# Three rotating PSUM tiles and eight score groups in an attention-plus-MLP kernel

## The chip, the core and the metric

The kernel runs on one core of a Trainium2 chip. The metric is device time in microseconds (us) of one execution. Five engines run their own instruction queues in order: TensorE (PE in the profile), VectorE (DVE), ScalarE (ACT), GpSimd (POOL) and SyncE (SP, which here only issues DMAs).

## The reference

Eight batches of 12 heads, 448 tokens, head size 64, go through an attention with normed q and k; its output, 3584 tokens of 768, goes through a two-layer MLP with a tanh GELU. Cut to what matters:

```python
def rmsnorm(x, g):
    return x / np.sqrt(np.mean(x * x, axis=-1, keepdims=True) + 1e-06) * g
scores = np.matmul(rmsnorm(q, g_q), rmsnorm(k, g_k).transpose(0, 1, 3, 2)) / np.sqrt(64)
attn = np.exp(scores - np.max(scores, axis=-1, keepdims=True))
attn = attn / (np.sum(attn, axis=-1, keepdims=True) + 1e-09)
x = np.matmul(attn, v).transpose(0, 2, 1, 3).reshape(8 * 448, 768)
h = x @ w_in                                    # 768 -> 2048
return gelu_tanh(h) @ w_out                     # 2048 -> 768
```

## The kernel before

The kernel walks over the batches. Everything is bf16 in the matmuls and float32 in PSUM. The instructions of each engine run in the order in which the Python code emits them (`manual_schedule`, L67); only waits between engines are added to it.

**Heads and units.** Twelve heads are three chunks `c` of four heads (`NCH = 3`). The 448 keys of a chunk are seven blocks `t` (`NT = 7`). A *unit* (L261) is one chunk and one block: four matmuls of 64x64 weights and 448 columns that run side by side in the four quarters of the array (a *set* below), which fill a PSUM tile `sc` of two banks, and one exponential on ACT (L274) that reads the tile and writes `ex[:, t]`. An attention has 21 units.

**Key sums.** The softmax sums go over keys. `key_sums` (L280) adds the `ex` blocks of a chunk on DVE: for the second block `es = ex0 + ex1` (L290), for the fourth and sixth `e2 = ex + ex` (L295) and `es += e2` (L296), for the seventh `es += ex` (L292). From batch 2 on all seven blocks are added so; for batch 1 chunks 0 and 2 add five, chunk 1 none. Then `products(b, c, 0)` (L298) multiplies what is left with ones on PE (one set where all was added), which gives the sums in a two-bank region `o`. `turned` (two transposes, L324) and `recips` (a reciprocal L330 and a transpose L331) turn them into `rb` on DVE.

**x.** `products(b, c, 1)` multiplies `v` with `ex` on PE (seven sets, also into `o`), and `quad_x` (L335) multiplies the result with `rb` on DVE into `xT`, one instruction per bank.

**The MLP.** `mm1` (L343) and `mm1_pair` (L404) make `h` from `xT` and `w_in` with 128x128 weights and 448 columns; ACT applies the GELU. `mm2` (L361) makes an output tile of 128 rows and 384 columns with 16 matmuls; the tile is then copied from PSUM by DVE (L391, `osb<-o`, called the *copy* below) and stored by SP.

**PSUM** has eight banks here: `ps_s` two tiles of two banks (`sc` and the pairs `hh` of the MLP, in turn), `ps_o` two banks (`o`, used by every sums and x product), `ps_m` two single banks (`mm`: `mm1`, `mm2`, transposes).

**The order in an attention** (L435) is written out: the 21 units go in 11 groups of two (the last has one), and a list `m2` of `mm2` matmuls of the batches before is dealt out between them: `first` 16 behind the first group, `last` 18 at the end, two beside each x product, the rest spread evenly, 112 in all (96 in the first such attention). After group 4 come the sums of chunk 0, after group 5 its x, after groups 8 and 9 those of chunk 1. Side work is hung to group numbers (`side`): sums of squares `total`, the gain of the keys `gain`, the inverse roots `rsqrt`, DMA issues. In each group the order of emission is: side work, units, the key sums of the previous group's second unit, a product, the `mm2` matmuls with their copies, and then the key sums of this group's first unit. At the end (L476 to L486) stand the last `mm2` matmuls, the sums of chunk 2, the first half of the MLP's first pair (`early`: inner chunks 0 to 3, which need the x of chunks 0 and 1), the x of chunk 2 and its multiplication, the second pair, and the `late` halves, which need the x of chunk 2. Then 72 `mm1` matmuls (L348) close the batch.

The very first attention (batch 0, `first_attention`, L488) has an order of its own. `attention` runs for batches 1 to 7.

Of the kernel before, what the change touches and what calls it, by code (L numbers as in the profile page):

```python
# [8 lines left out]
F32 = mybir.dt.float32  # L9
# [8 lines left out]
def kernel(  # L18
# [11 lines left out]
    nc = tc.nc  # L30
# [26 lines left out]
    xp = ctx.enter_context(tc.tile_pool(name="xp", bufs=2))  # L57
    gp = ctx.enter_context(tc.tile_pool(name="gp", bufs=1))
    op = ctx.enter_context(tc.tile_pool(name="op", bufs=3))
    ps_s = ctx.enter_context(tc.tile_pool(name="ps_s", bufs=2, space=bass.MemoryType.PSUM))  # L60
    ps_o = ctx.enter_context(tc.tile_pool(name="ps_o", bufs=1, space=bass.MemoryType.PSUM))
    ps_m = ctx.enter_context(tc.tile_pool(name="ps_m", bufs=2, space=bass.MemoryType.PSUM))

    ident = consts.tile([128, 128], BF16)
    make_identity(nc, ident)
# [190 lines left out]
    def gain(b, c):  # L256
        nc.vector.tensor_scalar(kT[:, c], kT[:, c], gcol[:, 0:1], None, op0=ALU.mult)
# [3 lines left out]
    def unit(b, c, t):  # L261

        if (b, c) not in exs:
            exs[b, c] = exq.tile([P, NT, 2, S], BF16, tag="ex", name="ex")
        ex = exs[b, c]
        sc = ps_s.tile([128, 2, 512], F32, tag="sc", name="sc")
        for a in range(2):
            rs = slice(a * D, (a + 1) * D)
            for r in range(2):
                nc.tensor.matmul(  # L270
                    sc[r * R:(r + 1) * R, a, :S], kT[rs, c, t, r], qT[b][rs, c, :, r],
                    start=True, stop=True,
                )
        nc.scalar.activation(ex[:, t], sc[:, :, :S], AF.Exp, scale=scale, bias=shift)  # L274
# [5 lines left out]
    def key_sums(b, c, t):  # L280

        n = added(b, c)
        if t > n or t == 0:
            return
        ex = exs[b, c]
        if t == 1:
            ess[b, c] = exq.tile([P, 2, S], BF16, tag="es", name="es")
        es = ess[b, c]
        if t == 1:
            nc.vector.tensor_add(es, ex[:, 0], ex[:, 1])  # L290
        elif t == n and n % 2 == 0:
            nc.vector.tensor_add(es, es, ex[:, t])  # L292
        elif t % 2:
            e2 = exq.tile([P, 2, S], BF16, tag="e2", name="e2")
            nc.vector.tensor_add(e2, ex[:, t - 1], ex[:, t])  # L295
            nc.vector.tensor_add(es, es, e2)  # L296

    def products(b, c, what, part=0, parts=1):  # L298

        if part == 0:  # L300
            oas[what] = [o[:, :S] for o in oall]
            if b == 0 and c + 1 == NCH and not what:
                oas[what] = [
                    ps_m.tile([128, 512], F32, tag="mm", name="os")[:, :S] for r in range(2)
                ]
        o = oas[what]
        es = [exs[b, c][:, t] for t in range(NT)]
        if not what and added(b, c):
            es[:added(b, c) + 1] = [ess[b, c]]
        n = len(es)  # L310
        for i in range(n * part // parts, n * (part + 1) // parts):
            for r in range(2):
                rs = slice(r * R, (r + 1) * R)
                for a in range(2):
                    nc.tensor.matmul(  # L315
                        o[r][a * D:(a + 1) * D],
                        vb[b % 2][rs, 2 * c + a, i] if what else ones[rs], es[i][rs, a],
                        start=(i == 0), stop=(i == n - 1),
                    )
# [15 lines left out]
    def quad_x(b, c):  # L335
        if c == 0:
            xT[b] = xp.tile([128, HP, S], BF16, tag="xT", name="xT")
        for r in range(2):
            nc.vector.tensor_mul(xT[b][:, 2 * c + r], oall[r][:, :S], oas["rb"][:, r])  # L339

# [63 lines left out]
    def mm1_pair(i, cs=range(HP), b=0, js=range(2)):  # L404

        if cs[0] == 0 and js[0] == 0:
            hs1[i] = ps_s.tile([128, 2, 512], F32, tag="sc", name="hh")
        h = hs1[i]
        for j in js:
            f = 2 * i + j  # L410
            for c in cs:
                nc.tensor.matmul(  # L412
                    h[:, j, :S], win[:, c, f * 128:(f + 1) * 128], xT[b][:, c],
                    start=(c == 0), stop=(c == HP - 1),
                )
        if cs[-1] == HP - 1 and js[-1] == 1:
            nc.scalar.activation(  # L417
                g[:, 2 * i:2 * i + 2, (b % 2) * S:(b % 2 + 1) * S], h[:, :, :S],
                AF.Gelu_apprx_tanh
            )  # L420
# [14 lines left out]
    def attention(b, m2, quota, side):  # L435

        units = [(c, t) for c in range(NCH) for t in range(NT)]
        groups = [units[i:i + 2] for i in range(0, len(units), 2)]
        first, last, beside = 16, 18, 2
        sums_at, x_at = {4: 0, 8: 1}, {5: 0, 9: 1}  # L440
        free = [i for i in range(1, len(groups) - 1) if i not in x_at]
        spread = quota - first - last - beside * len(x_at)
        given = 0

        def upto(k):
            nonlocal given
            while given < k:
                m2.pop(0)()
                given += 1

        before = []
        for i, group in enumerate(groups):
            for fn in side.get(i, ()):
                fn()
            for c, t in group:
                unit(b, c, t)
            for c, t in before:
                key_sums(b, c, t)
            if i in x_at:
                products(b, x_at[i], 1)  # L460
                quad_x(b, x_at[i])
                upto(given + beside)
            elif i in sums_at:
                products(b, sums_at[i], 0)
                turned()
            if i == 0:
                upto(first)
            elif i in free:
                n = spread * (free.index(i) + 1) // len(free) - spread * free.index(i) // len(free)
                upto(given + n // 2)  # L470
                if i in sums_at:
                    recips()
                upto(given + n - n // 2)
            key_sums(b, *group[0])
            before = group[1:]
        nc.scalar.preload_act_table_set(GELU_SET)  # L476
        upto(quota)

        c = NCH - 1
        products(b, c, 0)  # L480
        turned()
        mm1_pair(0, early, b)
        products(b, c, 1)
        recips()
        quad_x(b, c)
        mm1_pair(1, early, b)  # L486

# [166 lines left out]
    for b in range(B):  # L654
        m1, side = [], []
        if b == 0:

            m1 = [(0, lambda: total(1, 1, "q"),
                   lambda: total(1, 1, "k"), lambda: total(1, 2, "q"), lambda: total(1, 2, "k"),
                   lambda: rsqrt_newton(1), lambda: normed_both(1, 1, nc.gpsimd)),  # L660
                  (3, lambda: loads(2, 0)),
                  (4, lambda: transposed(1, 1), lambda: normed_both(1, 0, nc.vector),
                   lambda: normed_both(1, 2, nc.vector), lambda: loads(2, 1)),
                  (5, lambda: loads(2, 2),
                   lambda: square(2, 0, "q", nc.gpsimd),
                   lambda: square(2, 0, "k", nc.gpsimd)),
                  (5, lambda: trans(1, 0)),
                  (7, lambda: trans(1, 2))]
            side += [(0, lambda: total(2, 0, "q"), lambda: total(2, 0, "k")),
                     (2, lambda: gain(1, 1))]  # L670

            for c, slots in ((1, (5, 6)), (2, (7, 8))):
                for n, slot in zip("qk", slots):
                    side += [(2 * c - 1, lambda c=c, n=n: square(2, c, n, nc.gpsimd)),
                             (slot, lambda c=c, n=n: total(2, c, n))]
        elif b + 1 < B:

            m1.append((0, lambda: gpsimd_waits(ess[b, NCH - 1][:1, 0, :1])))
            for c in range(NCH):
                m1 += [(0, lambda c=c: normed_both(b + 1, c, nc.gpsimd)),  # L680
                       (4 * c + 4, lambda c=c: transposed(b + 1, c))]
            m1 += [(9, lambda: gain(b + 1, 0)), (14, lambda: gain(b + 1, 1))]
            side.append((3, lambda: gain(b + 1, 2)))
        if 0 < b and b + 2 < B:
            m1 += [(4, lambda: loads(b + 2, 1)), (8, lambda: loads(b + 2, 2))]
            for c, at in ((0, 4), (1, 9)):
# [22 lines left out]
            break  # L709
        nc.scalar.preload_act_table_set(EXP_SET)  # L710
        if b + 2 < B:
            side += [(10, lambda: rsqrt(b + 2)),
                     (0 if b else 2, lambda: load_v(b + 2, 0, HP))]
            if b + 3 < B:
                side.append((1, lambda: loads(b + 3, 0)))
        attention(b + 1, m2, 96 if b == 0 else 112, plan(*side))


# [28 lines left out]
```

## Time and profile before

| what | value |
|---|---|
| median of three runs | 425.52 us (425.33 to 425.61) |
| the profiled execution, its own time | 423.37 us |
| its span in the profile | 421.6 us |
| PE busy | 405.7 us, 96% of the span |
| ACT busy | 274.9 us, 65% |
| DVE busy | 259.8 us, 62% |
| POOL busy | 124.3 us, 29% |
| exponentials (L274) | 168, mean 1004 ns |
| copies of output tiles (L391) | 51, mean 550 ns |
| key-sum additions (L290, L292, L295, L296) | 116, 608 to 625 ns each |
| batch 2: its first units to those of batch 3 | 105.98 to 154.37 us |

The profile shows one execution. In its timeline view a line gives the start, the time, the engine, the line of the kernel, output and inputs, and how many instructions were merged; brackets give the idle time before it and what ended that. Matmuls overlap in the array, so the time from the start of one to the start of the next is what counts, not the time of one. The batches 2 to 7 repeat with a period of 48.39 us; batch 2 stands for them below.

### The profile page before, as it was taken

How to read it: one execution, taken by the hardware profiler on the slowest of the kernel's cores; microseconds unless marked ns; L12 is line 12 of the kernel's file. 1: busy time of each engine (PE TensorE's matmuls, PEld its weight loads, DVE VectorE, ACT ScalarE, POOL GpSimd, SP SyncE). 2: the span in 40 equal slices, each digit the busy share in tenths (PEclk: the TensorE clock that was granted, in tenths of full speed). 3: DMA queues.
4: the chain of work that ended last, by engine and by line, in shares of the span. 5: the costliest groups of instructions: out<-in, count | busy, mean ns of one | idle time of the engine just before them, and what ended most of it. 6: DMA issues, size and time to landing. Idle time of an engine off the chain costs nothing.

```text
span 421.6 us, 8029 instructions
## 1 busy us (share of the span) xinstructions
PE 405.7 (96%) x3321; PEld 205.7 (49%) x3321; DVE 259.8 (62%) x430; ACT 274.9 (65%) x364; POOL 124.3 (29%) x98
## 2 busy tenths in 40 slices
PE   5879999999999999999999999999999999999995
PEld 2336554545444544455444554445445454445563
DVE  4887947945689357973689455992589504891010
ACT  5885468838876587838877478747878348754300
POOL 5793515292202640063301840054400900000000
PEclk9998999999999999999999999999999999999999
DMA  7999999589521946249511958239411621130033
GB/s 261 208 256 243 218 192 280 96 205 264 78 62 41 241 79 181 76 104 294 98 39 39 215 129 191 64 83 268 64 46 39 125 45 38 39 75 3 0 75 76
DMA packets 65316, 54.06 MB, mean 128 GB/s; under 512 B 37376, under 2 KB 60288, under 8 KB 65280
## 3 DMA queue, kind: packets, MB, share of 16 engines
q1 hardware_dynamic: 52992, 41.66, 38.0%
q0 software_dynamic: 12128, 11.80, 17.7%
q8 instruction: 26, 0.43, 0.4%
q10 hardware_dynamic: 160, 0.10, 0.1%
q14 instruction: 10, 0.08, 0.1%
HBM read 45.61 MB, written 11.01 MB: 134 GB/s over the span
## 4 chain that ended last, share of the span: by engine, by line
PE 86%; ACT 9%; DVE 2%; POOL 2%; issue 1%; DMA 1%; DVEq 0%; ACTq 0%; POOLq 0%
PE o L368 32%; PE h L348 23%; PE hh L412 12%; PE o L315 9%; PE sc L270 8%; ACT ex L274 5%; ACT L710 2%; DVE ss L139 1%; POOL sq L134 1%; PE tp L228 1%; ACT g L354 1%; DMA rawq<-in_q_dram 1%; POOL win L544 1%; PE os L315 0%; DVE nrmk L210 0%
## 5 line engine op out<-in xcount | busy, mean ns | idle before, releaser
L274 ACT ACTIVATE ex<-sc,shift 128x896 bf16<-128x896 f32 x168 | 159.2, 1004 | 33.3 <-PE sc L270 31.9
L368 PE MATMUL o<-wout,g 128*128 128x384 bf16 x896 | 159.3, 327 | 0.0
L368 PEld LDWEIGHTS <-g 128*128 128x128 bf16 x896 | 81.3, 98 | 71.3 <-issue 23.3
L348 PE MATMUL h<-xT,win 128*128 128x448 bf16 x504 | 96.5, 352 | 0.0
L139 DVE TENSOR_REDUCE ss<-sq 128x14 f32<-128x896 f32 (+1 forms) x43 | 44.4, 1039 | 55.6 <-ACT sq L132 51.6
L348 PEld LDWEIGHTS <-win 128*128 128x128 bf16 x504 | 49.3, 98 | 46.0
L354 ACT ACTIVATE g<-h 128x448 bf16<-128x448 f32 x84 | 45.6, 543 | 28.2 <-PE h L348 23.1
L391 DVE COPY osb<-o 128x384 f32<-128x384 f32 x51 | 28.0, 550 | 58.3 <-PE o L368 58.0
L270 PE MATMUL sc<-qT,kT 64*64 64x448 bf16 x672 | 53.7, 366 | 4.7 <-ACT ex L274 3.5
L417 ACT ACTIVATE g<-hh 128x896 bf16<-128x896 f32 x22 | 19.3, 915 | 57.1 <-PE hh L412 57.1
L412 PE MATMUL hh<-xT,win 128*128 128x448 bf16 x264 | 52.9, 353 | 0.3 <-ACT g L417 0.3
L557 POOL COPY mark<-es 1x1 bf16<-1x1 bf16 x6 | 1.1, 177 | 139.7 <-DVE es L292 139.7
L210 POOL TENSOR_TENSOR nrmq<-rawq,rinv 128x896 bf16<-128x896 f32 x21 | 35.5, 1689 | 17.8 <-DVE o L195 11.9
L315 PE MATMUL o<-ex,vb 64*64 64x448 bf16 x672 | 38.1, 357 | 1.4 <-DVE st L324 1.4
L412 PEld LDWEIGHTS <-win 128*128 128x128 bf16 x264 | 24.6, 98 | 26.1 <-issue 5.0
L270 PEld LDWEIGHTS <-kT 64*64 64x64 bf16 x672 | 17.5, 104 | 37.1 <-issue 33.8
L210 POOL TENSOR_TENSOR nrmk<-rawk,rinv 128x896 bf16<-128x896 f32 x19 | 31.9, 1679 | 0.0
L324 DVE STREAM_TRANSPOSE st<-o 128x448 f32<-128x448 f32 x46 | 27.0, 625 | 6.8 <-PE o L315 6.7
L339 DVE TENSOR_TENSOR xT<-o,rb 128x448 bf16<-128x448 f32 x48 | 27.6, 618 | 4.7 <-PE o L315 4.2
L134 POOL TENSOR_TENSOR sq<-rawq 128x896 f32<-128x896 f32 x9 | 15.6, 1733 | 50.5 <-DVE ss L139 37.8
L315 PEld LDWEIGHTS <-vb 64*64 64x64 bf16 x672 | 20.4, 108 | 15.1 <-issue 4.6
L295 DVE TENSOR_TENSOR e<-ex 128x896 bf16<-128x896 bf16 x38 | 23.2, 611 | 7.0 <-ACT ex L274 7.0
(77 smaller groups left out, 266.0 us busy)
## 6 DMA issues: line engine op xcount, KB each, us to landing
out_dram<-osb SPq DMA_DIRECT2D x54, 192.0 KB, 2.7
rawq<-in_q_dram SPq DMA_DIRECT2D x23, 448.0 KB, 4.4
rawk<-in_k_dram SPq DMA_DIRECT2D x23, 448.0 KB, 4.9
vb<-in_v_dram POOLq DMA_DIRECT2D x8, 672.0 KB, 6.7
win<-in_moe_w_in_dram POOLq DMA_DIRECT2D x8, 384.0 KB, 13.7
wout<-in_moe_w_out_dram POOLq DMA_DIRECT2D x2, 1536.0 KB, 29.4
rawq<-in_q_dram SPq DMA_DIRECT2D x2, 224.0 KB, 2.6
rawk<-in_k_dram SPq DMA_DIRECT2D x2, 224.0 KB, 4.2
```

What stands on the lines that cost most here:

```text
L139: nc.vector.reduce_sum(sss[b][:, c, "qk".index(n), hs], sqs[n, b, c][:, hs], axis=AX.X)
L210: eng.tensor_mul(nrms[n, b, c][:, ts].rearrange("p t a d -> p a t d"), raws[n, b, c][:, :, ts], root[:, :, ts].to_broadcast([P, 2, m, D]),)
L270: nc.tensor.matmul(sc[r * R:(r + 1) * R, a, :S], kT[rs, c, t, r], qT[b][rs, c, :, r], start=True, stop=True,)
L274: nc.scalar.activation(ex[:, t], sc[:, :, :S], AF.Exp, scale=scale, bias=shift)
L315: nc.tensor.matmul(o[r][a * D:(a + 1) * D], vb[b % 2][rs, 2 * c + a, i] if what else ones[rs], es[i][rs, a], start=(i == 0), stop=(i == n ...
L324: nc.vector.transpose(st[:, r].rearrange("p a b -> p (a b)"), oas[0][r])
L339: nc.vector.tensor_mul(xT[b][:, 2 * c + r], oall[r][:, :S], oas["rb"][:, r])
L348: nc.tensor.matmul(h[:, :S], win[:, c, f * 128:(f + 1) * 128], xT[b][:, c], start=(c == 0), stop=(c == HP - 1),)
L354: nc.scalar.activation(g[:, f, (b % 2) * S:(b % 2 + 1) * S], h[:, :S], AF.Gelu_apprx_tanh)
L368: nc.tensor.matmul(o[:, :HD], g[:, f, i * 128:(i + 1) * 128], wout[:, f, half * HD:(half + 1) * HD], start=(f == 0), stop=(f == nf - 1),)
L391: nc.vector.tensor_copy(part, o[:, :HD])
L412: nc.tensor.matmul(h[:, j, :S], win[:, c, f * 128:(f + 1) * 128], xT[b][:, c], start=(c == 0), stop=(c == HP - 1),)
```

## The change

The PSUM pools `ps_s` and `ps_o` live until the first call of `attention` and are then closed; in their place come three tiles of two banks that go round in one fixed turn (`rounds`). Whoever asks for a two-bank tile (`pair`) gets the one whose last use lies furthest back: a unit's scores, a chunk's sums, a chunk's x, and the MLP pairs. `quad_x` then is one instruction over both banks.

The 21 units go in eight groups of 3, 3, 3, 2, 2, 3, 2 and 3. The sums of chunk 0 come after group 3, its x after group 4, the sums of chunk 1 after group 6. The x of chunk 1 moves to the end: there the sums of chunk 2, the x of chunk 1 and the x of chunk 2 follow one another on PE, and the first pair's early half comes behind them. 22 `mm2` matmuls stand behind the first group and 18 at the end; the rest is dealt evenly to the six groups between (12 each, 9 or 10 in the first such attention). At the end of a group the key sums of all its units but the last are emitted (in the last group those of the last unit too, ahead of the last 18 `mm2`). For chunk 2 the fifth, sixth and seventh blocks are added one by one. The group numbers of the side work are adapted: `gain(b + 1, 2)` from 3 to 2, `rsqrt` from 10 to 7, and in the first such attention `gain(1, 1)` from 2 to 1, the squares of batch 2 from 1 and 3 to 1 and 2, their totals from 5 to 8 to 4 to 6, and the load of `v` from 2 to 1.

```diff
-    ps_s = ctx.enter_context(tc.tile_pool(name="ps_s", bufs=2, space=bass.MemoryType.PSUM))
-    ps_o = ctx.enter_context(tc.tile_pool(name="ps_o", bufs=1, space=bass.MemoryType.PSUM))
     ps_m = ctx.enter_context(tc.tile_pool(name="ps_m", bufs=2, space=bass.MemoryType.PSUM))
+    start = ctx.enter_context(ExitStack())
+    ps_s = start.enter_context(tc.tile_pool(name="ps_s", bufs=2, space=bass.MemoryType.PSUM))
+    ps_o = start.enter_context(tc.tile_pool(name="ps_o", bufs=1, space=bass.MemoryType.PSUM))
+    rounds = []
+
+    def pair(name):
+        if not rounds:
+            return ps_s.tile([128, 2, 512], F32, tag="sc", name=name)
+        rounds.append(rounds.pop(0))
+        return rounds[-1]
...
-        sc = ps_s.tile([128, 2, 512], F32, tag="sc", name="sc")
+        sc = pair("sc")
...
-        elif t == n and n % 2 == 0:
+        elif t == n and n % 2 == 0 or c + 1 == NCH and t > 3:
             nc.vector.tensor_add(es, es, ex[:, t])
...
-        if part == 0:
+        if part == 0 and rounds:
+            o = oas["o", what] = pair("o")
+            oas[what] = [o[:, r, :S] for r in range(2)]
+        elif part == 0:
             oas[what] = [o[:, :S] for o in oall]
...
+        if rounds:
+            nc.vector.tensor_mul(
+                xT[b][:, 2 * c:2 * c + 2], oas["o", 1][:, :, :S], oas["rb"]
+            )
+            return
         for r in range(2):
             nc.vector.tensor_mul(xT[b][:, 2 * c + r], oall[r][:, :S], oas["rb"][:, r])
...
-            hs1[i] = ps_s.tile([128, 2, 512], F32, tag="sc", name="hh")
+            hs1[i] = pair("hh")
...
-        groups = [units[i:i + 2] for i in range(0, len(units), 2)]
-        first, last, beside = 16, 18, 2
-        sums_at, x_at = {4: 0, 8: 1}, {5: 0, 9: 1}
-        free = [i for i in range(1, len(groups) - 1) if i not in x_at]
-        spread = quota - first - last - beside * len(x_at)
+        cuts = (0, 3, 6, 9, 11, 13, 16, 18, 21)
+        groups = [units[i:j] for i, j in zip(cuts, cuts[1:])]
+        first, last = 22, 18
+        sums_at, x_at = {3: 0, 6: 1}, {4: 0}
+        between = len(groups) - 2
+        spread = quota - first - last
...
                 quad_x(b, x_at[i])
-                upto(given + beside)
...
-            elif i in free:
-                n = spread * (free.index(i) + 1) // len(free) - spread * free.index(i) // len(free)
+            elif i <= between:
+                n = spread * i // between - spread * (i - 1) // between
                 upto(given + n // 2)
                 if i in sums_at:
                     recips()
                 upto(given + n - n // 2)
-            key_sums(b, *group[0])
-            before = group[1:]
+            for c, t in group[:-1]:
+                key_sums(b, c, t)
+            before = group[-1:]
         nc.scalar.preload_act_table_set(GELU_SET)
+        for c, t in before:
+            key_sums(b, c, t)
         upto(quota)
 
         c = NCH - 1
         products(b, c, 0)
         turned()
-        mm1_pair(0, early, b)
+        products(b, c - 1, 1)
+        quad_x(b, c - 1)
         products(b, c, 1)
         recips()
+        mm1_pair(0, early, b)
         quad_x(b, c)
         mm1_pair(1, early, b)
...
+                     (1, lambda: gain(1, 1))]
+
+            for c, slots in ((1, (4, 5)), (2, (5, 6))):
                 for n, slot in zip("qk", slots):
-                    side += [(2 * c - 1, lambda c=c, n=n: square(2, c, n, nc.gpsimd)),
+                    side += [(c, lambda c=c, n=n: square(2, c, n, nc.gpsimd)),
...
-            side.append((3, lambda: gain(b + 1, 2)))
+            side.append((2, lambda: gain(b + 1, 2)))
...
-            side += [(10, lambda: rsqrt(b + 2)),
-                     (0 if b else 2, lambda: load_v(b + 2, 0, HP))]
+            side += [(7, lambda: rsqrt(b + 2)),
+                     (0 if b else 1, lambda: load_v(b + 2, 0, HP))]
...
+        if b == 0:
+            start.close()
+            ps_t = ctx.enter_context(
+                tc.tile_pool(name="ps_t", bufs=1, space=bass.MemoryType.PSUM))
+            rounds += [
+                ps_t.tile([128, 2, 512], F32, tag=f"t{i}", name=f"t{i}") for i in range(3)
+            ]
         attention(b + 1, m2, 96 if b == 0 else 112, plan(*side))
```

More of the change, by code (lines that the diff above doesn't have):

```diff
@@ L669 @@
             side += [(0, lambda: total(2, 0, "q"), lambda: total(2, 0, "k")),
-                     (2, lambda: gain(1, 1))]
-            for c, slots in ((1, (5, 6)), (2, (7, 8))):
+                     (1, lambda: gain(1, 1))]
+            for c, slots in ((1, (4, 5)), (2, (5, 6))):
                 for n, slot in zip("qk", slots):
-                    side += [(2 * c - 1, lambda c=c, n=n: square(2, c, n, nc.gpsimd)),
+                    side += [(c, lambda c=c, n=n: square(2, c, n, nc.gpsimd)),
                              (slot, lambda c=c, n=n: total(2, c, n))]
```

## The prediction

> **What bounds the kernel now.** I read the page's busy times and chain first, then batch 2, engine by engine, in the timeline; batches 3 to 7 repeat it.
>
> ```profile
> PE 405.7 (96%) x3321; PEld 205.7 (49%) x3321; DVE 259.8 (62%) x430; ACT 274.9 (65%) x364; POOL 124.3 (29%) x98
> PE 86%; ACT 9%; DVE 2%; POOL 2%; issue 1%; DMA 1%; DVEq 0%; ACTq 0%; POOLq 0%
> ```
>
> PE bounds: a microsecond matters if it is PE's. So the timeline of PE, the first groups and the end of batch 2's attention:
>
> ```profile
> 105.98 0.57 PE L270 MATMUL sc<-qT,kT 64*64 64x448 bf16 x8
> 106.48 2.77 PE L368 MATMUL o<-wout,g 128*128 128x384 bf16 x16
> 109.19 0.38 PE L270 MATMUL sc<-qT,kT 64*64 64x448 bf16 x4
> 109.89 0.38 PE L270 MATMUL sc<-qT,kT 64*64 64x448 bf16 x4 [0.33 <-ACT ex L274]
> 110.21 1.80 PE L368 MATMUL o<-wout,g 128*128 128x384 bf16 x10
> 111.94 0.57 PE L270 MATMUL sc<-qT,kT 64*64 64x448 bf16 x8
> 112.44 1.96 PE L368 MATMUL o<-wout,g 128*128 128x384 bf16 x11
> ...
> 134.23 0.38 PE L315 MATMUL o<-es,ones 64*64 64x448 bf16 x4
> 134.55 1.69 PE L412 MATMUL hh<-xT,win 128*128 128x448 bf16 x8
> 136.16 1.52 PE L315 MATMUL o<-ex,vb 64*64 64x448 bf16 x28
> ```
>
> PE waits once (109.89): two score tiles, and the fourth unit needs the second exponential. Everything else is matmuls end to end, but the 64x64 stretches cost more than their work. Ten mm2 and a pair of units take 110.21 to 112.44, eleven and a pair 112.44 to 114.84 (the next mm2): an mm2 is about 0.163. A set is 0.189 (448 columns, as the 72 matmuls of L348 in 13.63). So a pair's stretch, 2.23 - 10 x 0.1625 = 0.61, holds 0.38 of work and 0.23 of going over to 64x64 and back. The stretches here are 13: eleven groups and two at the end.
>
> VectorE matters next, since key sums release PE:
>
> ```profile
> 113.63 0.56 DVE L391 COPY osb<-o 128x384 f32<-128x384 f32 x1 [0.68 <-PE o L368]
> 114.11 0.45 DVE L257 TENSOR_SCALAR kT<-kT,gcols 128x896 bf16<-128x896 bf16 x1
> 114.47 0.62 DVE L295 TENSOR_TENSOR e<-ex 128x896 bf16<-128x896 bf16 x1
> 115.12 0.63 DVE L296 TENSOR_TENSOR es<-es,e 128x896 bf16<-128x896 bf16 x1
> 115.85 0.62 DVE L292 TENSOR_TENSOR es<-es,ex 128x896 bf16<-128x896 bf16 x1
> 117.37 1.18 DVE L324 STREAM_TRANSPOSE st<-o 128x448 f32<-128x448 f32 x2 [0.90 <-PE o L315]
> ```
>
> From start to start: copy 0.47, gain 0.36, e to es 0.65, es to a further es 0.73, an addition before something independent 0.54 (126.46 to 127.00). Chunk 0's key sums end at 116.47, PE takes them at 116.97: nothing waits. In batch 1 the queue shows its strict order: a gain waits 2.59 for a DMA, and the addition behind it, whose exponentials ended by 63.3, runs at 65.05.
>
> ```profile
> 64.68 0.45 DVE L257 TENSOR_SCALAR kT<-kT,gcols 128x896 bf16<-128x896 bf16 x1 [2.59 <-DMA kT<-nrmk]
> 65.05 0.62 DVE L295 TENSOR_TENSOR e<-ex 128x896 bf16<-128x896 bf16 x1
> ```
>
> **The change, part by part** (batch 2, on the same clock).
>
> *Fewer stretches.* Eight groups and one block at the end: 9 in place of 13, 4 x 0.23 = 0.93 saved. Row against page: the Trainium skill (TensorEngine Tiling (Array Packing), Key Properties) says a change of tiling mode drains TensorE, and TensorE: Matmul & The Clock Gate (Step-by-step) gives a drain some 128 cycles at 2.4 GHz, as an estimate 0.053, so 0.11 a stretch; by it the saving is 0.43 a batch and the whole result 3.5 us slower than mine (seven batches of 0.5). The trace's 0.23 decides.
>
> *The wait at the fourth unit* goes, 0.47 (109.89 less 109.19 and the 0.21 by which sets follow when a stretch begins): group 1 begins after three sets (0.21 and 0.19 apart), the way back to 128x128 (0.29), 22 mm2 (3.59) and the way out (0.09): 105.98 + 0.40 + 0.29 + 3.59 + 0.09 = 110.35. The exponentials that started at 107.94 end at 108.9, 109.8 and 110.7, when its three units need them. What is late next follows.
>
> *Exponentials.* Three follow in 0.9 + 0.89 + 1.0 (four took 3.70). Between starts of groups of three PE has 0.57 + 0.23 + 12 x 0.1625 = 2.75, ACT 2.69: it just keeps up. Unit 8 waits 0.10 for the tile of unit 5. rsqrt (0.62, ACT) falls in ACT's gap of 1 us before group 7.
>
> *Sums of chunk 0* (after group 3). PE is there at 116.40. The key sums of group 1's first units now stand behind all of the group's mm2, so behind the copy of the 32nd, which is the tenth of its twelve and ends at 112.87. From the copy on VectorE has: copy 0.47, e 0.66, es 0.54, gain 0.36 (moved in here), e 0.66, es 0.73, es 0.62: 112.91 + 4.04 = 116.95. PE waits to 117.00: 0.60. Between 110.6 and 112.9 VectorE is idle with nothing it may do.
>
> *Sums of chunk 1* (after group 6). The 80th mm2 is the tenth of group 5's twelve; its copy starts at 125.79, and the last key sum behind it ends 0.47 + 0.07 + 0.62 later, 126.94. PE was there at 126.40: 0.59. (Unit 15's exponential alone, whose tile the sums take, would hold it 0.13.)
>
> *Sums of chunk 2.* From those sums PE needs one set, 12 mm2, three units and 18 mm2 and stands ready at 133.09. VectorE, from the sums' end at 127.36: two transposes 1.20, reciprocal 0.36, rb 1.03, e 0.66, three es 0.73 each, the last 0.62: 133.46. PE waits 0.41; were VectorE free, the last exponential would still hold it 0.28 (129.36 + 0.44 + 2.80 + 0.77).
>
> *The end.* Product 1's seven sets only move here. Two copies queued behind the last key sum delay the transposes to 134.3; then x of chunk 1 ends at 136.56 (one instruction of 1.08 to 1.16 in place of two, by the 128x896 float32 rows), and PE needs it at 136.85. x of chunk 2 ends at 139.1, PE needs it at 139.5. Covers of 0.2 and 0.3; each tenth of VectorE delay beyond them is a tenth of PE time.
>
> *Costed at nothing:* later copies (the mm tiles are next written by mm1, 6 us on), SP's stores behind them, POOL's v load one or two groups earlier (0.88, POOL idle), other side work, the changed additions of chunk 2 (six before and after). Closing the pools could hold the first unit of batch 1 for both GELUs, 0 to 0.3 once; the table load until 59.13 covers it.
>
> Sum of a batch: -0.93 - 0.47 + 0.10 + 0.60 + 0.59 + 0.41 = +0.30, and four restarts of 0.02 (a set after a stall leads by 0.21, not 0.19): +0.38. Six batches: +2.3. The same laying out gives for batch 2 as it is 140.63 where the trace has 140.65.
>
> Batch 1: four stretches saved, 0.93; waits of now (three of 0.25, 0.21 at 69.79 for a weight DMA, 0.08) go; new are 0.2 at the first unit, 0.43 at unit 7 (the gain cannot run before its DMA, 65.1), 0.16, 0.39 and 0.62 at the sums: -0.1.
>
> Sum +2.1, on the profiled execution's 423.37 (421.6 of span, 1.8 around it) 425.5; that execution was 2.15 under the median, so against the runs 425.52 + 2.1 = **427.6**.
>
> **The unknown prices.** The new waits are the difference of two queues, so each bears the errors of both: how fast PE starts after an addition (0.05 by the one transpose-to-matmul row at 31.13; none, or 0.15 with a second semaphore), whether an addition may start 0.1 earlier or later. That makes +0.05 to +0.7 a batch, 0.3 to 4.2 in all; batch 1 -0.7 to +0.6. I stay with the middle, since the same spacings rebuild today's batch to 0.02.
>
> **Rivals.** *Faster: VectorE gets there in time.* If the key sums of chunks 0 and 1 were ready 0.6 earlier, only 0.02 and 0.13 of the two waits stay, 0.28 of the third: -0.85 a batch, 425.52 - 5.2 = 420.3. For it: VectorE is 62% busy. Against: both chains begin at a copy that PE's own pace sets. It decides where the waits sum to under 1.4 a batch.
>
> *Slower still: ScalarE becomes the bound.* In batch 1 four exponentials took 3.82 to 3.86, 0.95 apart. At that pace three take 2.85 against PE's 2.75, and each of four groups of three plus its release adds 0.1 to 0.2: some 0.3 a batch more, 429.7. Against: the 3.86 rows have a PE round trip through two tiles in each step. The Trainium skill's TensorEngine Tiling (Array Packing), PSUM Bottleneck, warns of just that: tiling speeds TensorE, not the emptying of PSUM. The trace of batch 2 does not bear it out: ScalarE idles 0.33 to 0.74 before each pair.
>
> *No difference:* savings and waits cancel, 425.5; it needs three of the four waits to be a tenth shorter each.
>
> **Chances.** Forecast 0.62 (426.4 to 429.2), faster rival 0.14, ScalarE rival 0.10, no difference 0.14. A measurement of this kernel tells 0.2% (0.85) from nothing. So faster 0.14, same 0.14, slower 0.72. The range, 424.7 to 430.0, leaves out the faster rival and the far tail.
>
> **What would show it.** Right: in batch 2 no wait of PE at the fourth unit; PE waits of 0.4 to 0.6 for VectorE at the two single sums and before the x block at the end; a copy ahead of the additions that end there; stretches of three units that cost 0.80 (two cost 0.61); the batch's period 48.8. Wrong: sums without waits (period 47.5), PE waits put down to exponentials at units 6, 8, 14 or 16, a stretch that costs 0.11, or a wait of the first MLP pair for x of chunk 1.

## The result and the profile after

| | before | after |
|---|---|---|
| median of 16 runs | 425.28 us | 426.84 us |
| lowest to highest | 423.12 to 427.92 | 425.61 to 429.67 |
| the profiled execution, its own time | 423.37 us | 429.09 us |
| its span | 421.6 us | 427.0 us |
| first units of batch 2 to those of batch 3 | 48.39 us | 48.75 us |

The change makes the kernel slower: the ratio after to before is 1.0048, with an interval of 1.0027 to 1.0069, so 1.1 to 2.9 us; the two medians lie 1.56 us apart. The prediction had +2.1 us in all, and +0.38 us for a batch where the traces show 48.75 - 48.39 = +0.36.

The two profiled executions lie 5.7 us apart, the medians 1.56, so the spans must be split before they are read. The first units of batch 1 start at 57.58 before and at 61.20 after: +3.62. From there to the first units of batch 2 (105.98 and 109.17) it is 48.40 before and 47.97 after: -0.43. From there to the end it is 315.62 and 317.83: +2.21, six times 0.37. Of the 3.62 at the start 0.22 belong to the change; 3.29 were lost before the first exponential (11.54 and 14.83) in code that is the same in both kernels (last section), and 0.11 between the two is not accounted for. Between these two executions the change then makes 0.22 - 0.43 + 2.21 = +2.0 us. The -0.43 belongs to a batch 1 that begins as late as after's did; e2 below shows one that begins early.

The page of after, busy times and the shares of the chain that ended last:

```profile
PE 402.6 (94%) x3321; PEld 211.4 (50%) x3321; DVE 260.3 (61%) x409; ACT 273.2 (64%) x364; POOL 124.3 (29%) x98
PE 73%; DVE 17%; ACT 4%; issue 2%; POOL 2%; DMA 1%; DVEq 0%; ACTq 0%; POOLq 0%
```

The number of matmuls is the same, and PE's busy time is 3.1 us lower. But VectorE has risen from 2% to 17% of the chain: PE now stands waiting for it. The waits view of after, for PE, says where (us in total, times, longest):

```profile
PE t L328 <- DVE es L302: 7.1, 18, 0.5
```

Eighteen waits: three in each of the batches 2 to 7, for the sums of the three chunks, each for a key sum (`es`) of VectorE. Before had no such line. Its largest wait for exponentials, 3.5 us in nine times, is 1.6 in three now, all in batch 0, and 1.2 in three of batch 1. PE in batch 2, in the timeline of after:

```profile
109.17 0.76 PE L280 MATMUL t<-qT,kT 64*64 64x448 bf16 x12
109.86 3.75 PE L386 MATMUL o<-wout,g 128*128 128x384 bf16 x22
113.54 0.83 PE L280 MATMUL t<-qT,kT 64*64 64x448 bf16 x12
...
116.35 0.86 PE L280 MATMUL t<-qT,kT 64*64 64x448 bf16 x12
117.15 2.13 PE L386 MATMUL o<-wout,g 128*128 128x384 bf16 x12
119.20 0.57 PE L280 MATMUL t<-qT,kT 64*64 64x448 bf16 x8
120.23 0.38 PE L328 MATMUL t<-es,ones 64*64 64x448 bf16 x4 [0.45 <-DVE es L302]
...
129.23 0.57 PE L280 MATMUL t<-qT,kT 64*64 64x448 bf16 x8
130.16 0.38 PE L328 MATMUL t<-es,ones 64*64 64x448 bf16 x4 [0.36 <-DVE es L302]
...
133.22 3.10 PE L386 MATMUL o<-wout,g 128*128 128x384 bf16 x18
136.69 0.38 PE L328 MATMUL t<-es,ones 64*64 64x448 bf16 x4 [0.37 <-DVE es L302]
...
139.65 4.71 PE L430 MATMUL t<-xT,win 128*128 128x448 bf16 x24
```

Three units stand together at 109.17, and nothing waits at the fourth (113.54): that wait is gone. The stretch of three takes 0.69 (109.17 to 109.86), at unit 5 0.76 and at unit 8 0.80. A sums product that doesn't wait follows its pair of units after 0.40 (two units, 0.21 and 0.19). At 120.23 it comes 1.03 after the pair, 0.63 late; at 130.16 0.53 late; before the one at 136.69 stand 18 `mm2` and the way out, which in before take 3.03 without a wait (131.20 to 134.23) and here 3.47 (133.22 to 136.69), so it comes 0.44 late. The idle time in brackets is shorter, because the modelled end of a matmul lies behind the time at which the next could begin (0.57 is shown for a pair of units that the sums can follow after 0.40). The first MLP pair (139.65) runs through without a wait for the x of chunk 1. VectorE in the same time, in the timeline of after:

```profile
116.14 0.56 DVE L409 COPY osb<-o 128x384 f32<-128x384 f32 x1 [2.37 <-PE o L386]
116.61 0.61 DVE L305 TENSOR_TENSOR e<-ex 128x896 bf16<-128x896 bf16 x1
117.26 0.63 DVE L306 TENSOR_TENSOR es<-es,e 128x896 bf16<-128x896 bf16 x1
117.81 0.45 DVE L267 TENSOR_SCALAR kT<-kT,gcols 128x896 bf16<-128x896 bf16 x1
...
119.55 0.62 DVE L302 TENSOR_TENSOR es<-es,ex 128x896 bf16<-128x896 bf16 x1
...
129.01 0.56 DVE L409 COPY osb<-o 128x384 f32<-128x384 f32 x1 [1.52 <-PE o L386]
129.49 0.61 DVE L302 TENSOR_TENSOR es<-es,ex 128x896 bf16<-128x896 bf16 x1
```

VectorE idles 2.37 for the copy of an output tile that PE hasn't finished, and then does in a row what PE is waiting for: copy, two additions, the gain, three additions, 116.14 to 120.17, and PE starts at 120.23. The same at 129.01: 1.52 idle, copy, one addition. A busy share of 61% hides this; that the order in the queue decides is shown by e1.

### The profile page after: what moved, and what is told of

The parts are those of the page before. It is cut to its first block, busy times and chain, and to the rows that moved or that the text cites. A ratio compares the mean times of both kernels' runs of the same rounds, so it can differ in the third digit from the quotient of the medians.

```text
span 427.0 us, 8035 instructions
## 1 busy us (share of the span) xinstructions
PE 402.6 (94%) x3321; PEld 211.4 (50%) x3321; DVE 260.3 (61%) x409; ACT 273.2 (64%) x364; POOL 124.3 (29%) x98
## 4 chain that ended last, share of the span: by engine, by line
PE 73%; DVE 17%; ACT 4%; issue 2%; POOL 2%; DMA 1%; DVEq 0%; ACTq 0%; POOLq 0%
PE o L386 23%; PE h L366 22%; PE t L328 8%; PE t L430 8%; DVE es L302 4%; PE t L280 4%; PE hh L430 4%; ACT ex L284 3%; DVE es L306 3%; DVE e L305 2%; DVE st L337 2%; DVE rb L344 2%; PE o L328 1%; DVE osb L409 1%; POOL sq L144 1%
## 5 line engine op out<-in xcount | busy, mean ns | idle before, releaser
L284 ACT ACTIVATE ex<-t,shift 128x896 bf16<-128x896 f32 x147 | 137.4, 1006 | 31.7 <-PE t L280 31.1
L386 PE MATMUL o<-wout,g 128*128 128x384 bf16 x896 | 155.5, 327 | 0.0
L435 ACT ACTIVATE g<-t 128x896 bf16<-128x896 f32 x14 | 12.1, 914 | 46.0 <-PE t L430 46.0
L280 PE MATMUL t<-qT,kT 64*64 64x448 bf16 x588 | 39.9, 360 | 0.7 <-ACT ex L284 0.5
L430 PE MATMUL t<-xT,win 128*128 128x448 bf16 x168 | 33.0, 353 | 0.0
L328 PE MATMUL t<-ex,vb 64*64 64x448 bf16 x588 | 30.3, 349 | 0.0
L328 PEld LDWEIGHTS <-vb 64*64 64x64 bf16 x672 | 23.0, 109 | 11.3 <-issue 2.0
L344 DVE STREAM_TRANSPOSE rb<-rc 128x896 f32<-128x896 f32 x24 | 26.7, 1111 | 0.8
L337 DVE STREAM_TRANSPOSE st<-t 128x448 f32<-128x448 f32 x42 | 24.8, 628 | 1.5 <-ACT ex L284 1.0
L352 DVE TENSOR_TENSOR xT<-t,rb 128x896 bf16<-128x896 f32 x21 | 22.6, 1078 | 1.3 <-DVE rb L344 0.5
```

Of the source, the lines that this page charges most:

```text
L280: nc.tensor.matmul(sc[r * R:(r + 1) * R, a, :S], kT[rs, c, t, r], qT[b][rs, c, :, r], start=True, stop=True,)
L328: nc.tensor.matmul(o[r][a * D:(a + 1) * D], vb[b % 2][rs, 2 * c + a, i] if what else ones[rs], es[i][rs, a], start=(i == 0), stop=(i == n ...
L337: nc.vector.transpose(st[:, r].rearrange("p a b -> p (a b)"), oas[0][r])
L344: nc.vector.transpose(rb.rearrange("p r s -> p (r s)"), rc.to_broadcast([128, 2 * S // 32, 32]))
L386: nc.tensor.matmul(o[:, :HD], g[:, f, i * 128:(i + 1) * 128], wout[:, f, half * HD:(half + 1) * HD], start=(f == 0), stop=(f == nf - 1),)
L430: nc.tensor.matmul(h[:, j, :S], win[:, c, f * 128:(f + 1) * 128], xT[b][:, c], start=(c == 0), stop=(c == HP - 1),)
```

## The experiments

The theory: fewer stretches save 0.23 each and the third tile takes the wait at the fourth unit away, but PE now waits for key sums that stand in VectorE's queue behind a copy which PE itself makes late. Rivals: VectorE has too much to do at these places whatever the order; ScalarE's pace sets the sums; a stretch costs less than 0.23 (0.11), and something else holds the batch. The times of e1 to e4 were taken beside 14 runs of before (median 424.52), those of e5 to e7 beside 11 (425.44).

### e1: the key sums ahead of the copy

After, with the key sums of a group's first units emitted after the first half of its `mm2`, ahead of the copy that falls into the second half.

```diff
                 upto(given + n // 2)
                 if i in sums_at:
                     recips()
+                for c, t in group[:-1]:
+                    key_sums(b, c, t)
                 upto(given + n - n // 2)
-            for c, t in group[:-1]:
-                key_sums(b, c, t)
+            if not 0 < i <= between:
+                for c, t in group[:-1]:
+                    key_sums(b, c, t)
             before = group[-1:]
```

> The changed kernel, but in the groups between the first and the last the key sums of a group's first units are emitted after the first half of its mm2 matmuls, ahead of the copy that stood before them. If VectorE's order is what holds PE at the single sums, the waits of chunks 0 and 1 fall from 0.5 each to about 0 and 0.1, and the one at the end stays near 0.4 to 0.5: the period of batches 2 to 7, 48.39 before and 48.75 after the change, becomes 47.8, and the whole run about 6 us shorter than the changed kernel, 421 to 422. If ScalarE were the bound behind it, PE would wait for exponentials in place of the sums, and the period would stay above 48.5.

Measured: period 47.87 (107.61 to 155.48), 422.18 us against 424.52, ratio to before 0.9923 (0.9895 to 0.995). VectorE of e1, in the timeline:

```profile
113.45 0.62 DVE L305 TENSOR_TENSOR e<-ex 128x896 bf16<-128x896 bf16 x1 [1.25 <-ACT ex L284]
...
114.66 0.55 DVE L409 COPY osb<-o 128x384 f32<-128x384 f32 x1
...
116.86 0.63 DVE L302 TENSOR_TENSOR es<-es,ex 128x896 bf16<-128x896 bf16 x1
```

and PE of e1:

```profile
117.64 0.57 PE L280 MATMUL t<-qT,kT 64*64 64x448 bf16 x8
118.09 0.38 PE L328 MATMUL t<-es,ones 64*64 64x448 bf16 x4
...
127.09 0.57 PE L280 MATMUL t<-qT,kT 64*64 64x448 bf16 x8
127.63 0.38 PE L328 MATMUL t<-es,ones 64*64 64x448 bf16 x4
```

The same instructions, the same number of them: the first block now waits for its exponential instead of for the copy, the last key sum ends at 117.49 and PE, there at 118.04, takes the sums at 118.09. The wait of 0.63 is 0.05, that of 0.53 is 0.14 (127.09 to 127.63, less 0.40). Only the third stays (134.25, 0.52 late). For chunks 0 and 1 VectorE's load is not the cause, its order is: there the rival "too much to do" falls. For chunk 2 it does not: no run moves its additions, and in after VectorE is never idle from the copy at 129.01 to the last of them, which ends at 136.63, while the last exponential has ended by 135.76. The whole run, 422.18, is just above the 421 to 422 that were expected.

### e2: the gain one group later

After, with `gain(b + 1, 2)` back in group 3, which takes 0.36 of VectorE out of the chain ahead of chunk 0's key sums and nothing else.

```diff
-            side.append((2, lambda: gain(b + 1, 2)))
+            side.append((3, lambda: gain(b + 1, 2)))
```

> The changed kernel with the gain of chunk 2's keys put back from group 2 to group 3, so that VectorE has 0.36 less to do between the copy and the key sums of chunk 0. If the wait there is the plain sum of VectorE's queue, it shrinks by 0.36 and nothing else moves: period 48.4 in place of 48.75. If PE waited for the exponential or its tile instead, the period stays at 48.75.

Measured: period 48.39 (107.45 to 155.84), and 425.21 us in one run. The timeline of PE in e2:

```profile
117.48 0.57 PE L280 MATMUL t<-qT,kT 64*64 64x448 bf16 x8
118.15 0.38 PE L328 MATMUL t<-es,ones 64*64 64x448 bf16 x4
...
128.08 0.38 PE L328 MATMUL t<-es,ones 64*64 64x448 bf16 x4 [0.35 <-DVE es L302]
```

The sums of chunk 0 are 0.27 late instead of 0.63, the batch 0.36 shorter: what leaves VectorE's chain there leaves the batch, one to one. The sums of chunk 1 are 0.53 late as in after (127.15 to 128.08, less 0.40). If ScalarE set the sums, the gain's place would not matter.

This run shows one thing more, in batch 1, whose order is the same as in after. It begins at 57.95 here, at 61.20 in after's profile. The waits view of e2 has two lines that after's has not:

```profile
PE o L386 <- DMA wout<-in_moe_w_out_dram: 1.3, 1, 1.3
PE t L280 <- DVE kT L267: 1.0, 1, 1.0
```

Both lie in batch 1: PE idles 0.97 until 65.93, where unit 7 waits for the gain, which itself waited 2.88 for its DMA, and 1.28 until 71.82 for the DMA of a weight. Batch 1 takes 49.50 (57.95 to 107.45) where after's took 47.97. So what the change costs in batch 1 depends on when that batch begins, and the +2.0 of the two profiles is not the cost for every execution.

### e3: two more stretches

After, with the third unit of the first group put in the middle of the 22 `mm2`, and three `mm2` of group 4 put into its x product. The same work; two more turns from 128x128 to 64x64 and back.

```diff
                 unit(b, c, t)
+                if i == 0 and t == 1:
+                    upto(first // 2)
...
-                products(b, x_at[i], 1)
+                products(b, x_at[i], 1, 0, 2)
+                upto(given + 3)
+                products(b, x_at[i], 1, 1, 2)
...
+                n -= 3 if i in x_at else 0
```

> The changed kernel with two more 64x64 stretches in each attention of batches 1 to 7: the third unit of group 0 stands in the middle of the 22 mm2 matmuls, and the x product of chunk 0 is cut in two by three mm2 matmuls. Same matmuls, same order of everything else. At 0.23 a stretch the period grows by 0.46 to 49.2; at the 0.11 that the page's drain gives, to 48.97.

Measured: period 49.15 (105.26 to 154.41), 0.40 over after; 427.55 us in one run. The first group and the x product of chunk 0 in the timeline of e3:

```profile
105.26 0.57 PE L280 MATMUL t<-qT,kT 64*64 64x448 bf16 x8
...
109.87 0.76 PE L280 MATMUL t<-qT,kT 64*64 64x448 bf16 x12
...
119.26 0.74 PE L328 MATMUL t<-ex,vb 64*64 64x448 bf16 x12
...
121.40 1.64 PE L386 MATMUL o<-wout,g 128*128 128x384 bf16 x9
```

The waits were 1.69 in e3's batch against 1.78 in after's (by the same reading; the table below), so the two turns cost 0.40 + 0.09 = 0.49, 0.24 or 0.25 each. Seen directly: the first group with its 22 `mm2` takes 4.61 (105.26 to 109.87) where after has 4.37 (109.17 to 113.54), 0.24 for this turn. For the other, from the x product's start to the next stretch of `mm2` there are 28 matmuls in seven sets and three `mm2`, 119.26 to 121.40, 2.14; in after the seven sets to the next `mm2` take 123.00 to 124.43, 1.43, and three `mm2` are 0.49; 2.14 - 1.43 - 0.49 = 0.22. The 0.23 of the prediction lies between; the price of 0.11 falls.

### e4: the three tiles alone

Before, with the first half of the change only: three tiles in turn, and `quad_x` in one instruction. Groups of two, all places and the side work stay as they were; so there are 13 stretches.

```diff
+    def pair(name):
+        if not rounds:
+            return ps_s.tile([128, 2, 512], F32, tag="sc", name=name)
+        rounds.append(rounds.pop(0))
+        return rounds[-1]
...
-        sc = ps_s.tile([128, 2, 512], F32, tag="sc", name="sc")
+        sc = pair("sc")
```

> The kernel before with the three rotating tiles and the one-instruction x alone: groups of two, products, mm2 matmuls, key sums and side work all where they were. If tiles and regrouping pay and cost as I laid out, only the wait at the fourth unit (0.47) goes and no new one comes: period 47.9, the run about 3 us shorter than before. If the shared tiles themselves made PE wait (a sums or x tile still being read when its turn comes), the period would stay at 48.4 or above.

Measured: period 47.87 (107.66 to 155.53), 421.79 us against 424.52, ratio to before 0.9921 (0.9893 to 0.9949). PE of e4, in the timeline:

```profile
110.87 0.57 PE L280 MATMUL t<-qT,kT 64*64 64x448 bf16 x8
...
117.74 0.57 PE L280 MATMUL t<-qT,kT 64*64 64x448 bf16 x8
118.14 0.36 PE L328 MATMUL t<-es,ones 64*64 64x448 bf16 x4
```

Units 3 and 4 (110.87; the next `mm2` follows at 111.38) run through, the sums come 0.40 after their pair, and no wait of PE is left in the batch: 0.52 saved, of which the fourth unit's wait is 0.47; the other 0.05 is not accounted for. The tiles bring none of the new waits; the new groups, with the order of the key sums that came with them, save four stretches more (0.92) and pay 1.78 in waits: 48.75 - 47.87 = 0.88 a batch lost.

### e5: the three tiles, and x of chunk 1 at the end

e4, with the x of chunk 1 moved between the sums and the x of chunk 2, as in after; one stretch fewer, groups of two.

```diff
-        sums_at, x_at = {4: 0, 8: 1}, {5: 0, 9: 1}
+        sums_at, x_at = {4: 0, 8: 1}, {5: 0}
...
         turned()
-        mm1_pair(0, early, b)
+        products(b, c - 1, 1)
+        quad_x(b, c - 1)
         products(b, c, 1)
         recips()
+        mm1_pair(0, early, b)
```

> The kernel with three tiles alone, groups of two, and besides the x of chunk 1 moved to the end as in the change. It saves one more 64x64 stretch (0.23) and should bring no wait of note (0.03 at the sums of chunk 0): period 47.7 in place of 47.87. If the end could not bear the x product (PE waiting for x of chunk 1 or 2 there), the period stays at 47.87 or above, with a wait of the first MLP pair for VectorE.

Measured: period 47.71 (105.28 to 152.99), 419.85 us against 425.44, ratio to before 0.9881 (0.9853 to 0.991). The end of batch 2's attention, PE of e5:

```profile
131.97 2.82 PE L328 MATMUL t<-ex,vb 64*64 64x448 bf16 x56
134.72 4.71 PE L430 MATMUL t<-xT,win 128*128 128x448 bf16 x24
```

The x of two chunks in one block costs no wait when the last key sums are in time: 0.16 a batch saved by this step, against 0.23 for the stretch; 0.04 of the rest is a wait at the sums of chunk 0. So this move, taken alone, pays. The run is 1.2% faster than before.

### e6 and e7: the `mm2` dealt anew

e6 is e1 with 20 `mm2` first, 20 last and 5 beside the x product, the rest spread over the other five groups (and in the group of the x product the key sums come behind the five `mm2`); it lengthens the groups in which PE waited and gives the end more cover. e7 is e1 with 20 last instead of 18 and nothing else.

```diff
-        first, last = 22, 18
+        first, last, beside = 20, 20, 5
...
```

> Eight groups with the key sums ahead of the copies, and the mm2 matmuls dealt out anew: 20 behind the first group, 20 at the end, five beside the x product of chunk 0, the rest evenly. Laid out from the rows: a wait of 0.33 at unit 5 comes back, the one before the end shrinks from 0.5 to 0.2, the ones at the sums go: period 47.6. If the exponentials bind in the groups that get more matmuls taken away, PE waits at units 6, 8 or 15 and the period stays above 47.87.

> Eight groups with the key sums ahead of the copies and 20 in place of 18 mm2 matmuls at the end. The wait before the end falls from 0.5 to 0.26, as the PE comes later, but two matmuls fewer between the groups make unit 8 wait 0.26 in place of 0.10 for its exponential: period 47.7, 0.13 under 47.87. If the wait at the end were bound by the last exponential and not by VectorE's queue, it would fall by all of 0.33.

Measured: e6 47.52 (106.18 to 153.70), 419.99 us against 425.44, ratio to before 0.989 (0.9859 to 0.9922); e7 47.68 (108.04 to 155.72), 421.59 in one run. PE of e6, in the timeline:

```profile
110.23 0.57 PE L280 MATMUL t<-qT,kT 64*64 64x448 bf16 x8
111.00 0.38 PE L280 MATMUL t<-qT,kT 64*64 64x448 bf16 x4 [0.20 <-ACT ex L284]
111.32 2.29 PE L386 MATMUL o<-wout,g 128*128 128x384 bf16 x13
```

and of e7:

```profile
115.07 1.02 PE L280 MATMUL t<-qT,kT 64*64 64x448 bf16 x12
116.02 2.12 PE L386 MATMUL o<-wout,g 128*128 128x384 bf16 x12
...
134.49 0.38 PE L328 MATMUL t<-es,ones 64*64 64x448 bf16 x4 [0.17 <-DVE es L302]
```

Two more `mm2` at the end cut the wait there from 0.52 to 0.24 in e7, and take a matmul from group 1. The three units of group 2 behind it then wait 0.26 (the stretch is 0.95 instead of 0.69), while ScalarE runs its exponentials without a gap (110.01 to 118.35). In e6 the wait at unit 5 is 0.40 and the end's 0.18. Here ScalarE's pace is what comes next: where fewer `mm2` stand ahead of a group of three (20 in place of 22 at unit 5, 11 in place of 12 at unit 8), PE waits for it longer. With the key sums ahead of the copies and the `mm2` dealt so, the eight groups give the shortest batch of all, 0.35 under e4: the groups, too, pay once VectorE's order fits them. The runs of e6 are no shorter than those of e5 all the same; in the profiles batch 1 takes 47.99 in e6 (1.05 of it a wait for the gain) and 47.48 in e5, which is part of it.

### One ledger for all

Three terms give the period of batch 2 in each kernel: a base, 0.23 for each stretch over nine, and the waits of PE read from its timeline as above (stretch of three less 0.69, sums less 0.40, the end less 3.03, or 3.35 where 20 `mm2` stand there). The base, 46.95, comes from e4, which has no wait: 47.87 less 4 x 0.23.

| kernel | stretches | units | sums 0 | sums 1 | end | base + terms | measured |
|---|---|---|---|---|---|---|---|
| before | 13 | 0.47 | 0 | 0 | 0 | 48.34 | 48.39 |
| after | 9 | 0.18 | 0.63 | 0.53 | 0.44 | 48.73 | 48.75 |
| e1 | 9 | 0.17 | 0.05 | 0.14 | 0.52 | 47.83 | 47.87 |
| e2 | 9 | 0.17 | 0.27 | 0.53 | 0.44 | 48.36 | 48.39 |
| e3 | 11 | 0.17 | 0.56 | 0.52 | 0.44 | 49.10 | 49.15 |
| e5 | 12 | 0 | 0.04 | 0 | 0 | 47.68 | 47.71 |
| e6 | 9 | 0.40 | 0 | 0 | 0.18 | 47.53 | 47.52 |
| e7 | 9 | 0.32 | 0.01 | 0.14 | 0.24 | 47.66 | 47.68 |

The waits of units are those at the fourth unit in before and at units 5 and 8 elsewhere. No kernel misses by more than 0.05. What stays open is why a turn costs 0.23: the runs give its price, not its parts.

## Why the prediction was right

- **Fewer stretches, -0.93.** Right: e3 gives 0.22 to 0.25 for a turn, the ledger holds with 0.23 for kernels of 9, 11, 12 and 13 stretches. The Trainium skill's price (TensorE: Matmul & The Clock Gate, Step-by-step: a drain of 128 cycles; from it the prediction's estimate of 0.11 a stretch) is not what these runs show; by it the two turns of e3 would cost 0.22, where they cost 0.46 to 0.49.
- **The wait at the fourth unit, -0.47.** Right: gone in after and in e4, where 0.52 came off the batch.
- **Units of later groups, +0.10.** Low by a little: 0.11 at unit 8, and 0.07 at unit 5, which was thought free.
- **Sums of chunk 0, +0.60.** 0.63, by the chain named: copy at 116.14, then 4.03 on VectorE where 4.04 was laid out. e1 shows that the place behind the copy is the cause, e2 that the moved gain is 0.36 of it.
- **Sums of chunk 1, +0.59.** 0.53. The copy at 129.01 and one addition behind it; e1 leaves 0.14, the 0.13 of unit 15's tile.
- **Sums of chunk 2, +0.41.** 0.44. From the sums of chunk 1 to these it is 6.53 in after and e2 and 6.62 in e1, where the two other waits are all but gone, so the chain of VectorE behind the sums of chunk 1 sets it and not what came before. (The spacings listed for it in the prediction add up to 133.42 and not 133.46, which would make it 0.37.)
- **The end, 0.** Right: the first MLP pair runs through at 139.65.
- **Sum of a batch.** New waits 1.78 where 1.70 and 0.08 of restarts stood; +0.36 against +0.38.
- **Batch 1, -0.1** (its listed terms add up to -0.17). In the profile -0.43 and 0.22 at its first unit, so -0.2, but this is in part luck. The 0.43 at unit 7 did not come, since batch 1 began late and the gain's DMA had landed; unit 8 waited 0.63 instead of 0.16, and the two misses cancel. In e2, where batch 1 began early, the wait for the gain was there, larger than forecast (0.97 idle), and so was one of 1.28 for a weight DMA, which the prediction took to go. The sums of chunks 0 and 1 waited 0.41 and 0.63 in after, for exponentials, where 0.39 and 0.62 stood.
- **The rivals.** "VectorE gets there in time" asked for key sums of chunks 0 and 1 some 0.6 earlier; that came only in e1, by another order: period 47.87 and 0.9923 of before, where after stands at 1.0048. "ScalarE becomes the bound" did not come: its mean exponential is 1006 ns (1004 before), and the waits for it are 0.18 a batch.

The total of 1.1 to 2.9 by the runs holds the +2.1; the medians alone, 1.56 apart, make it somewhat high. That the two profiles give +2.0 hangs on the late start of after's batch 1. What the profiled execution lost at the start, 3.29, was in no term, and the medians don't show it. The six equal batches, +0.36 against +0.38 each, are where the mechanism was forecast and met.

## What to carry to other kernels

Where two engines feed each other, lay out the queue of the one that is only 60% busy: an addition that PE waits for must not stand behind a copy that PE itself delays, and moving it half a group forward was worth 0.9 us a batch here. When a change has two parts (here tiles, and groups with a new order), run one alone: the tiles alone took 0.52 off a batch, the groups, in the order they came with, saved 0.92 and cost 1.78. A price found from two spacings of one trace (0.23 for a turn) can carry a prediction, if an experiment that adds two of them confirms it.

## What the runs showed of the hardware

**VectorE instructions take longer beside POOL's squares.** Small products of VectorE in the start-up of after, in its timeline:

```profile
6.82 2.47 DVE L595 TENSOR_TENSOR gprod<-grow 64x32 f32<-64x32 f32 x2
9.64 1.27 DVE L597 TENSOR_SCALAR gdiag<-ident,gcols 64x64 bf16<-64x64 bf16 x1
```

and POOL of after at that time:

```profile
7.57 1.68 POOL L144 TENSOR_TENSOR g<-rawq 128x896 f32<-128x896 f32 x1
9.20 1.68 POOL L144 TENSOR_TENSOR g<-rawk 128x896 f32<-128x896 f32 x1
```

The same products in the timeline of before:

```profile
6.91 0.77 DVE L572 TENSOR_TENSOR gprod<-grow 64x32 f32<-64x32 f32 x2
8.04 0.23 DVE L574 TENSOR_SCALAR gdiag<-ident,gcols 64x64 bf16<-64x64 bf16 x1
```

There POOL's square waited 0.95 for a DMA until 8.38, and `gdiag` (0.23) ended before it began. In after the data was there and the square followed without a gap: the two products took 2.47 and ended as the first square did (9.29 and 9.25), `gdiag` took 1.27 and ended as the second did (10.91 and 10.88). PE waits for `gdiag`. Over the nine profiles of this study the two go together: where `gdiag` took 1.22 to 1.55 (after, e1, e4, e7; POOL's square at 7.57 to 7.96), batch 1 began at 59.62 to 61.20; where it took 0.23 (before, e2, e3, e5, e6; the square at 8.38 to 8.66), at 56.47 to 58.19. The code up to there is the same in all; which of the two comes goes with when the DMA of POOL's input lands. In batch 1 it is seen again, VectorE of after:

```profile
67.04 1.13 DVE L305 TENSOR_TENSOR e<-ex 128x896 bf16<-128x896 bf16 x1 [0.89 <-ACT ex L284]
68.21 1.99 DVE L306 TENSOR_TENSOR es<-es,e 128x896 bf16<-128x896 bf16 x1
```

with POOL of after:

```profile
65.87 1.82 POOL L144 TENSOR_TENSOR sq<-rawq 128x896 f32<-128x896 f32 x1 [8.42 <-DVE es L300]
67.65 2.06 POOL L144 TENSOR_TENSOR sq<-rawk 128x896 f32<-128x896 f32 x1
```

Additions of 0.62 elsewhere take 1.13 and 1.99, and each ends 0.5 after a square does (68.17 and 67.69, 70.20 and 69.71), as if it had begun only then; POOL's squares of 1.68 take 1.82 and 2.06. The Trainium skill (SBUF — State Buffer, Who interferes with whom) says that a VectorE instruction with two inputs in SBUF and a GpSimd instruction that reads SBUF contend for a shared port, which one of them holds for its whole instruction while the other is blocked. The rows of `gprod` and of the additions agree with it; `gdiag` multiplies a tile by a column, a form that this sentence does not name. No experiment here moved POOL's squares, so that this is the cause of the late start is argued, not shown.

**A lower clock is the other part.** PE's product behind `gdiag` starts 2.65 later in after than in before (10.97 and 8.32). The other 0.64 of the 3.29 come behind it: from 11 to 14 us the granted clock of TensorE was 0.50 in after and 1.00 in before, and the same seven transposes took 0.95 and 0.55. In the nine profiles the clock fell to 0.50 in this stretch in all but before and e3, and these two have the earliest first exponentials, 11.54 and 11.66, against 12.49 to 14.83. What makes it fall is not shown here: e5 had it after PE had idled 1.26, before did not after 2.51.

For a reader of profiles it means that a few microseconds between two single executions can arise at the start, far from the change: compare stretches, not spans.
